# Storing weight blocks earlier and in larger pieces, and loading shared keys once, in a fused attention and MLP kernel

## The chip, the cores and the metric

The kernel runs on one core of a Trainium2 chip. The metric is device time in microseconds of one execution, as a median of several. TensorE (PE), VectorE (DVE), ScalarE (ACT), GpSimd (POOL) and SyncE (SP) each run their instructions in the order in which they were written into the program; SP does nothing here but issue transfers.

## The reference

Chunked attention, with 4 batches, 8 heads, 768 positions and 64 columns a head, is followed by a two-layer MLP over the 3072 tokens.

```python
for c in range(S // 32):                 # chunks of 32 queries
    lo, hi = max(0, 32*c - 16), min(S, 32*c + 32 + 8)
    k_full = concat([mem_k, k[:, :, lo:hi]])      # 8 memory keys and up to 56 neighbours
    a = softmax(q_c @ k_full.T / 8)               # + 1e-9 in the denominator
    out_c = a @ concat([mem_v, v[:, :, lo:hi]])
x = out.reshape(3072, 512)
y = (s * relu(x @ w_in)**2 + b) @ w_out           # 512 -> 2048 -> 512
```

Inputs and outputs are fp32 (the weights arrive as 64-bit floats and are cut down on the chip). Products are formed from a high and a low part of each operand, with three matmuls for one product.

## The kernel before, in words

**Attention.** A *visit* handles six pairs of (block of 64 queries, pair of heads). It loads `raw` (queries and keys, line 506) and `v` (values, line 511), makes scores on TensorE (line 520), takes maxima and exponentials (lines 595 and 599), normalizes on POOL (608 to 611), transposes (632 on DVE, or 620 on TensorE for early visits) and multiplies with the values (line 559). There are 32 visits; each block carries its own copy of its 96 keys, 88 of its window and 8 of memory, so that a pair takes 64 + 96 columns. Visits 0 to 11 serve three token groups of 384; the other 20 serve two groups of 960 tokens, and their results are stored to `xs` (line 570).

**First MLP part.** 48 steps, each with 12 matmuls of the first layer (`hidden`, line 677) and 9 of the second (`result`, line 707), run over the three small token groups. Meanwhile the 32 weight tiles are loaded, decoded and cut into high and low parts (lines 648 to 662), and stay in SBUF.

**Second MLP part.** The two groups of 960 tokens use Strassen-Winograd products: `seven` (line 896) for the first layer and `rest` (line 1018) for the second, once for each group. They need blocks of the weights (A11, A12, A22) and sums of blocks (S1 to S4). These are put together in DRAM, in `w1s` and `w2s`, as 56 *words* each, and a word holds two blocks with their high and low parts, 512 KB. `whole_blocks` lists 48 stores of single blocks (256 KB each); `save` (line 755) issues three of them after each step above 24. `blocks` makes the four sums of a pair of weight tiles on POOL (lines 766 and 774), cuts them on ACT and DVE (777 and 778), and stores them (line 784) with one transfer of 128 KB for each sum and part, eight for a pair of tiles and 128 in all. The buffers `words` (four) hold the sums until their stores have landed. Both kinds of store read `all_w`, the last weight tiles, so none starts before the weights are done. `word` (line 874) reads the words back. `mix` makes the operands B11, B21, B22 and T1 to T4 of each large group from `xs` (loads on line 835, cuts on lines 845 and 846, subtractions on 850).

**Order.** The program is written out by a planner. Each operation has an engine, a holding time and a priority, which is a step number plus an entry of the table `NUDGE`; a list scheduler lays them out against a model of the engines and of the transfers (sizes over `RATE`, at most `FLIGHT` = 8 in flight). What comes out is the fixed order of each engine's instructions. All transfers but one are on SP's queue, in that order.

Of the kernel before, what the change touches and what calls it, by code (L numbers as in the profile page):

```python
# [11 lines left out]
F32 = mybir.dt.float32  # L12
# [9 lines left out]
B, H, S, D = 4, 8, 768, 64  # L22
# [18 lines left out]
QKB = QB + KB  # L41
# [6 lines left out]
LATER = 24.0  # L48
LATE_SUMS = 3
NUDGE = {  # L50
# [69 lines left out]

KINDS = list(dict.fromkeys(k for _, combos in VIEWS for k in kinds_of(combos)))
AT_V = 1024
# [4 lines left out]
BLOCKS = ("A11", "S2", "S1", "S3", "A12", "S4", "A22")  # L127
# [17 lines left out]
STORE, ROWS = 0.85, 1.2  # L145
# [200 lines left out]
def body(ctx: ExitStack, tc: tile.TileContext, qkv, w1, w2, out):  # L346
    nc = tc.nc
    dram = ctx.enter_context(tc.tile_pool(name="dram", bufs=1, space=bass.MemoryType.DRAM))
    w1s = [dram.tile([P, 2, 2, 2 * P], F32, name=f"w1s{i}") for i in range(NWORDS)]
    w2s = [dram.tile([P, 2, 2, 2 * P], F32, name=f"w2s{i}") for i in range(NWORDS)]  # L350
# [35 lines left out]
    raws = ring("raw", 2, [P, GP * QKB], F32)  # L386
# [95 lines left out]
    def attend(vis):  # L482
# [4 lines left out]
        nj, qk, tok = nb // 2, nb * QKB, nb * QB  # L487
# [5 lines left out]
        if vis >= H // 2:  # L493
            raw, v = Val(raws), Val(vs_)
        else:
            raw = Early(NEARLY - 1 - c, 0, GB * QKB)
            v = Early(NEARLY - 5 - c, 0, 2 * GB * D)
# [3 lines left out]
        pieces = (3, 3)[vis] if vis < 2 else 1  # L501
        piece = lambda j: raw[j * pieces // nj]
        first = (lambda: raw.tile) if vis else (lambda: early_tiles[NEARLY - 1])
        for n in range(pieces):
            lo, hi = n * qk // pieces, (n + 1) * qk // pieces + 2 * (not vis and n == pieces - 1)
            op("SP", "issue", a - 4 + load, lambda lo=lo, hi=hi: nc.sync.dma_start(first()[:, lo:hi], qkv[vis][:, lo:hi]), (), (raw[n],),
               size=ROWS * P * (hi - lo) * 4)
# [6 lines left out]
        def product(j):  # L514

            for u in range(2):
                lo = (2 * j + u) * QKB
                for n in range(2):
                    rows = slice(n * D, (n + 1) * D)
                    nc.tensor.matmul(scv(n, j)[u * QB:(u + 1) * QB], raw.tile[rows, lo:lo + QB], raw.tile[rows, lo + QB:lo + QKB],  # L520
                                     start=True, stop=True)
# [40 lines left out]
        def store():  # L562
            if ch is None:
                op("ACT", "xhigh", due + late, lambda: nc.scalar.activation(x.tile[:, :tok], av(), AF.Copy), (va[0],), (x[0],))
                cs, gg = [list(dict.fromkeys(k[i] for k in combos)) for i in range(2)]
                p, lo = divmod(gg[0] - NPLAIN * GB, PB)
                lo, n = lo * QB, len(gg) * QB
                key, i = (p, cs[0] // 2), cs[0] % 2
                staged[key].append((lo, lo + n, vis))
                op("SP", "issue", due + late, lambda: nc.sync.dma_start(  # L570
                    xs[key][:, i:i + len(cs), lo:lo + n], x.tile[:, :tok].rearrange("q (c t) -> q c t", c=len(cs))), (x[0],),
                   (c_xs[key][vis],), size=ROWS * P * tok * 4)
                return
            op("ACT", "xhigh", due + late, lambda: nc.scalar.activation(x.tile[c][:, 0], av(), AF.Copy), (va[0],), (x["H", c],))
            op("DVE", "xlow", due + late, lambda: nc.vector.tensor_tensor(x.tile[c][:, 1], av(), x.tile[c][:, 0].bitcast(F32), ALU.subtract),
               (va[0], x["H", c]), (x["L", c],))
# [93 lines left out]
    def hidden(u):  # L670
# [25 lines left out]
        if u > LATER:  # L696
            save(u, o)

    def result(u):
# [9 lines left out]
        for t in range(NT):  # L709
# [17 lines left out]
            op("SP", "issue", u, lambda ot=ot, row=row: nc.sync.dma_start(out[row:row + P, :], ot()), (o[0],), (), size=ROWS * P * DM * 4)  # L727
# [6 lines left out]
    def save(u, after):  # L734

        for side, unit, q, fn, reads in keep[:3]:
            o = op("SP", "issue", u, fn, reads, (c_ws[side][unit][q, 0],), size=STORE * P * 4 * P * 4)
            o.deps.add(after)
        del keep[:3]
# [4 lines left out]
    def whole_blocks(side, g):  # L744

        fs = (2 * g, 2 * g + 1)
        parts = [[c_w[side, f]["H"], c_w[side, f]["L"]] for f in fs]
        for name in BLOCKS:
            if name in SUMS:
                continue  # L750
            unit, q = place(side, g, name)
            i, k = int(name[1]) - 1, int(name[2]) - 1
            if side:
                i, k = k, i
            keep.append((side, unit, q, lambda unit=unit, q=q, i=i, k=k: nc.sync.dma_start(  # L755
                (w1s, w2s)[side][unit][:, q], weight_tile(side, fs[i])[:, :, k * 2 * P:(k + 1) * 2 * P].bitcast(F32)), [*parts[i], *all_w]))

    def blocks(side, g, due):
# [21 lines left out]
        for name in SUMS:  # L780
            unit, q = place(side, g, name)
            i = where[name]
            for a, v in enumerate((high, sums)):
                op("SP", "issue", due + 0.5, lambda unit=unit, q=q, a=a, v=v, i=i: nc.sync.dma_start(  # L784
                    (w1s, w2s)[side][unit][:, q, a], at(v, i)), (v[0] if v is high else v[i],), (c_ws[side][unit][q, a],), size=STORE * P * 2 * P * 4)
# [82 lines left out]
    def word(p, n, prio):  # L868
        v = Val(streams)
        side, unit = divmod(n, NWORDS)  # L870
        src, c_src = (w1s, w2s)[side][unit], c_ws[side][unit]
        gone = first("stream", stream_slots)
        flat = src.rearrange("p a b n -> p (a b n)")
# [5 lines left out]
    def seven(p, g):  # L879
# [30 lines left out]
        b5 = product("P5", "S1", "T1", 2)  # L910
        sz = Val(wvs, "sz")
        op("DVE", "addp", due - AHEAD, lambda: nc.vector.tensor_tensor(sb(sz), pt(b5), sb(su), ALU.add), (b5[0], su[0]), (sz[0],))
        b7 = product("P7", "S3", "T3", 3)
# [19 lines left out]
    def rest(p):  # L933
# [39 lines left out]
        def out_(m, i, k, due, bank, v=None, add=None, parts=1):  # L973
# [14 lines left out]
            for x in range(parts):  # L988
# [3 lines left out]
                    dst[at:at + P, lo:hi], o.tile[:, lo:hi]), (o[x],), (), size=ROWS * P * (hi - lo) * 4)  # L992
# [143 lines left out]
```

## Time and profile before

| | |
|---|---|
| median of 3 runs | 583.51 us |
| lowest and highest | 582.13 and 585.71 us |
| the profiled execution's own time | 585.3 us |
| its span, first to last instruction | 583.5 us |
| mean granted TensorE clock | 0.994 |
| busy share | PE 98%, DVE 73%, ACT 67%, POOL 34% |
| moved by DMA | 148.08 MB |

The span is what the trace resolves; 1.8 us of the profiled execution's time lie outside it. The profiled execution is near the slow end of the three runs. A step of the first MLP part is a unit of the planner's priorities.

### The profile page before, as it was taken

To read this page: it belongs to the slowest core of one execution; us is meant where nothing else is said; L and a number is where in the kernel's file an instruction comes from. 1 tells how busy PE (TensorE), PEld (TensorE's weight loads), DVE (VectorE), ACT (ScalarE), POOL (GpSimd) and SP (SyncE) were. 2 spreads that over 40 slices of the span, in tenths; PEclk is the share of its full clock that TensorE was granted. 3 is DMA by queue.
4 is the path that set the end of the run, shared out by engine and by line. 5 is a ranking of instruction groups with operands and counts; after the bars stand their busy time and mean duration, and the time that the engine had idled before them with its cause. 6 is when DMAs were issued, how large, how long until landed. Compare 5 with 4: busy or idle time off the path is not lost.

```text
span 583.5 us, 11567 instructions
## 1 busy us (share of the span) xinstructions
PE 570.3 (98%) x3963; PEld 485.5 (83%) x3963; DVE 424.5 (73%) x1117; ACT 393.1 (67%) x950; POOL 196.9 (34%) x230
## 2 busy tenths in 40 slices
PE   7999999999999999899999999999999999999997
PEld 4688888988888788688888888888888888888886
DVE  5889899647968577958988577999734434399653
ACT  6899999667785577857587857675525564655552
POOL 4466354877743468610782212000000101100000
PEclk9999999999999999979999999999999999999999
DMA  8967665148999999996999978767776656666761
GB/s 293 405 256 258 234 211 177 38 154 265 338 328 357 366 308 314 332 322 248 317 370 335 309 243 278 231 213 223 238 262 206 212 189 208 192 205 192 242 215 67
DMA packets 71386, 148.08 MB, mean 254 GB/s; under 512 B 7072, under 2 KB 43808, under 8 KB 71328
## 3 DMA queue, kind: packets, MB, share of 16 engines
q1 hardware_dynamic: 71184, 147.23, 75.4%
q8 instruction: 31, 0.51, 0.4%
q14 instruction: 27, 0.22, 0.1%
q10 hardware_dynamic: 144, 0.12, 0.1%
HBM read 107.74 MB, written 39.58 MB: 252 GB/s over the span
## 4 chain that ended last, share of the span: by engine, by line
PE 78%; DMA 7%; DVE 4%; ACT 3%; SPq 3%; POOL 2%; issue 1%; DVEq 0%; POOLq 0%; ACTq 0%
PE ps L896 25%; PE ps L1018 25%; PE ps L677 11%; PE ps L707 11%; DMA w1s<-w 5%; PE ps L559 3%; PE ps L520 2%; ACT t L599 2%; DVE aT L632 1%; SPq L755 1%; POOL words L774 1%; DMA v<-qkv 1%; DMA w1s<-words 1%; POOL t L611 1%; SPq L784 1%
## 5 line engine op out<-in xcount | busy, mean ns | idle before, releaser
L896 PE MATMUL ps<-again,again 128*128 128x480 f32 x672 | 148.8, 381 | 0.0
L896 PEld LDWEIGHTS ps<-again,again 128*128 128x128 f32 x672 | 125.6, 188 | 20.8
L677 PE MATMUL ps<-x,w 128*128 128x384 f32 x576 | 112.8, 343 | 0.3 <-POOL w L662 0.3
L677 PEld LDWEIGHTS ps<-x,w 128*128 128x128 f32 x576 | 102.3, 191 | 5.9 <-POOL w L662 0.6
L707 PE MATMUL ps<-w,gH 128*128 128x512 f32 x288 | 90.2, 394 | 0.0
L599 ACT ACTIVATE t<-t,nmax 128x96 f32<-128x96 f32 x192 | 69.6, 366 | 19.0 <-DVE nmax L595 18.5
L1018 PE MATMUL ps<-gH,again 128*128 128x482 f32 x272 | 81.5, 380 | 0.0
L632 DVE STREAM_TRANSPOSE aT<-t 32x192 f32<-32x192 f32 x192 | 70.6, 368 | 13.2 <-POOL t L611 10.3
L707 PEld LDWEIGHTS ps<-w,gH 128*128 128x128 f32 x288 | 54.2, 188 | 10.3
L1018 PE MATMUL ps<-again,again 128*128 128x482 f32 x264 | 62.0, 382 | 0.0
L707 PE MATMUL ps<-w,gL 128*128 128x512 f32 x144 | 58.8, 408 | 1.2 <-DVE gL L694 1.1
L1018 PEld LDWEIGHTS ps<-gH,again 128*128 128x128 f32 x272 | 51.3, 188 | 8.2
L1018 PEld LDWEIGHTS ps<-again,again 128*128 128x128 f32 x264 | 49.7, 188 | 8.1
L774 POOL TENSOR_TENSOR words<-words 128x256 f32<-128x256 f32 x64 | 48.0, 750 | 12.3 <-DVE words L778 6.9
L1018 PE MATMUL ps<-gL,again 128*128 128x482 f32 x136 | 51.7, 380 | 0.0
L766 POOL TENSOR_TENSOR words<-w 128x512 f32<-128x512 f32 x32 | 41.3, 1303 | 23.7 <-DMA w1s<-words 17.4
L595 DVE CUSTOM_DVE_ANT_0 t<-ps,mask 128x96 f32<-128x96 f32 x192 | 38.2, 252 | 14.1 <-PE ps L520 13.5
L662 POOL TENSOR_TENSOR w<-wv,w 128x512 fp32r<-128x512 f32 x28 | 36.2, 1298 | 32.4 <-ACT w L659 17.0
L611 POOL TENSOR_TENSOR t<-t,rden 128x576 f32<-128x576 f32 (+1 forms) x40 | 39.2, 982 | 16.8 <-DVE rden L610 8.0
L694 DVE TENSOR_TENSOR gL<-ps,gH 128x384 fp32r<-128x384 f32 x48 | 26.5, 552 | 19.8 <-ACT gH L693 19.5
L692 ACT ACTIVATE ps<-ps,b_sb,s_sb 128x384 f32<-128x384 f32 x48 | 30.6, 638 | 11.4 <-DVE ps L688 10.6
L931 POOL TENSOR_TENSOR againx<-againx 128x480 f32<-128x480 f32 x4 | 5.4, 1348 | 95.6 <-ACT againx L930 89.2
(105 smaller groups left out, 894.6 us busy)
## 6 DMA issues: line engine op xcount, KB each, us to landing
again<-w1s SPq DMA_DIRECT2D x56, 512.0 KB, 4.5
again<-w2s SPq DMA_DIRECT2D x56, 512.0 KB, 4.2
raw<-qkv SPq DMA_DIRECT2D x28, 480.0 KB, 5.3
words<-w SPq DMA_DIRECT2D x24, 512.0 KB, 4.6
v<-qkv SPq DMA_DIRECT2D x28, 384.0 KB, 5.4
w1s<-words SPq DMA_DIRECT2D x64, 128.0 KB, 3.4
w2s<-words SPq DMA_DIRECT2D x64, 128.0 KB, 4.4
w1s<-w SPq DMA_DIRECT2D x24, 256.0 KB, 5.0
```

The source lines that it names most:

```text
L595: op("DVE", "max", a + 0.1, lambda j=j: nc.vector.tensor_tensor_reduce(t.tile[:, n, j, :], scv(j), mask[:, kinds[j]], -SCALE, 3.0e38, ALU. ...
L599: op("ACT", "exp", a + 0.2, lambda j=j: nc.scalar.activation(t.tile[:, n, j, :], t.tile[:, n, j, :], AF.Exp, bias=nmax()[:, j:j + 1], scal ...
L611: op("POOL", NORM[len(each)], a + 0.25, lambda: nc.gpsimd.tensor_tensor(t.tile[:, heads, :nj], t.tile[:, heads, :nj], rden().unsqueeze(3). ...
L632: nc.vector.transpose(aT.tile[gg, :, :nj, u, c * CHUNK:(c + 1) * CHUNK], t.tile[rows, :, :nj, gg])
L662: op(low, "vsum" if turn_ else "wjoin", due, lambda: e.tensor_tensor(dst(1), v.tile, dst(0).bitcast(F32), ALU.subtract), (v[0], w["H"]), ( ...
L677: nc.tensor.matmul(h.tile[:, :TOK], weight_tile(0, f)[:, wi, c * P:(c + 1) * P], x.tile[c][:, xi], start=(c == 0 and n == 0), stop=(c == N ...
L692: op("ACT", "affine", u - ahead, lambda: nc.scalar.activation(hp(), hp(), AF.Identity, scale=s_sb, bias=b_sb), (c_s[0], c_b[0]), (h[0],))
L707: nc.tensor.matmul(acc.tile, g.tile[gi][:, t * P:(t + 1) * P], weight_tile(1, f)[:, wi, :], start=(first and n == 0), stop=(last and n == 2))
L766: o = op("POOL", "vsum", due, lambda k=k, f=f: nc.gpsimd.tensor_tensor(at(sums, 2 * k, 2), weight_tile(side, f)[:, 0].bitcast(F32), weight ...
L774: op("POOL", "ssum", due, lambda to=to, a=a, b=b, how=how: nc.gpsimd.tensor_tensor(at(sums, to), at(sums, a), at(sums, b), how), [sums[x] ...
L896: nc.tensor.matmul(bank.tile[:, :PT], w.tile[:, lo:lo + P], xv.tile[xi][:, kc], start=(not more and kc == 0 and i == 0), stop=(kc == 1 and ...
L1018: nc.tensor.matmul(sx(bank), w.tile[:, lo:lo + P], cut.tile[xi], start=(first and k == 0), stop=(last and k == 2), skip_group_check=True)
```

## The change

- `raw` packs runs of neighbouring blocks: first the queries of a run, then its keys, of which each block after the first adds only `STEP` = 72 columns (64 and the memory keys). Blocks read overlapping windows of 96 columns. A visit of six blocks in one run has 840 columns (one of two runs of three has 864) instead of 960; visits 0 and 1 are loaded in three runs of two blocks, of 296 columns instead of 320.
- `save` begins at step 14 instead of 25 and issues two stores after a step instead of three.
- The sums go out two or three at a time: for a pair of second-layer tiles S2, S3 and S4 together and S1 alone; for the first layer two and two, or two, one and one. With both parts that is 4 or 6 transfers instead of 8, and 72 instead of 128 in all. For this `w1s` becomes tiles of seven words and `w2s` one tile of 56, and the order of blocks in a first-layer word list swaps S1 and S3.
- `seven` computes product P7 ahead of P5.
- The planner's sizes of transfers lose their factors (1.2 for rows, 0.85 for stores; 1.3 stays on the loads of `mix`), and `NUDGE` is a new table, so that the order on every engine is new.

```diff
+STEP = QB + NMEM
+SAVE, NSAVE = 14, 2
 NUDGE = {
-    ('a', 0): -0.5, ('a', 10): -6, ...  ('m', 1): -4.5, ...
+    ('a', 0): -0.5, ('a', 1): 4.5, ...  ('m', 0): 0.5, ('m', 1): 3.75, ...
 }
+def places(vis):
+    runs = []
+    for i, (c, g) in enumerate(VIEWS[vis][1]):
+        if vis < 2 and i % 2 == 0 or not i or VIEWS[vis][1][i - 1] != (c, g - 1):
+            runs.append([])
+        runs[-1].append(i)
+    q, k, ends, at = {}, {}, [], 0
+    for run in runs:
+        for n, i in enumerate(run):
+            q[i], k[i] = at + n * QB, at + len(run) * QB + n * STEP
+        at = k[run[-1]] + KB
+        ends.append(at)
+    return q, k, ends
-BLOCKS = ("A11", "S2", "S1", "S3", "A12", "S4", "A22")
+BLOCKS = ("A11", "S2", "S3", "S1", "A12", "S4", "A22")
-STORE, ROWS = 0.85, 1.2
+ROWS = 1.3
-    w1s = [dram.tile([P, 2, 2, 2 * P], F32, name=f"w1s{i}") for i in range(NWORDS)]
-    w2s = [dram.tile([P, 2, 2, 2 * P], F32, name=f"w2s{i}") for i in range(NWORDS)]
+    stored = [[dram.tile([n, P, 2, 2, 2 * P], F32, name=f"w{side + 1}s{i}") for i in range(NWORDS // n)] for side, n in ((0, len(BLOCKS)), (1, NWORDS))]
...
-                    nc.tensor.matmul(scv(n, j)[u * QB:(u + 1) * QB], raw.tile[rows, lo:lo + QB], raw.tile[rows, lo + QB:lo + QKB],
+                    nc.tensor.matmul(scv(n, j)[u * QB:(u + 1) * QB], raw.tile[rows, q:q + QB], raw.tile[rows, k:k + KB],
...
-        if u > LATER:
+        if u >= SAVE:
             save(u, o)
...
-        for side, unit, q, fn, reads in keep[:3]:
+        for side, unit, q, fn, reads in keep[:NSAVE]:
...
-        for name in SUMS:
-            unit, q = place(side, g, name)
-            i = where[name]
+        pairs = (("S2", "S3", "S4"), ("S1",)) if side else (("S2", "S4"), ("S3", "S1")) if g % 2 == 0 else (("S2", "S4"), ("S3",), ("S1",))
+        for names in pairs:
+            to, at_ = [place(side, g, n) for n in names], [where[n] for n in names]
+            (u, q), n, step = to[0], len(names), at_[1] - at_[0] if len(names) > 1 else 1
+            t, u = words_at(side, u)
             for a, v in enumerate((high, sums)):
+                if n > 1 and to[1][0] == to[0][0]:
+                    dst = t[u, :, :, a]
+                elif n > 1:
+                    by = to[1][0] - to[0][0]
+                    dst = t[u:u + by * (n - 1) + 1:by, :, q, a].rearrange("u p n -> p u n")
...
-        b5 = product("P5", "S1", "T1", 2)
+        b7 = product("P7", "S3", "T3", 2)
+        b5 = product("P5", "S1", "T1", 3)
...
-        b7 = product("P7", "S3", "T3", 3)
```

## Rows read from the trace of the kernel before

**Rows 1.** Windows by stage: PE, PEld, DVE, ACT, POOL busy; clock, DMA share, GB/s.

```profile
0.00:32.00 32.00, 27.85 (x347) 18.55 (x348) 23.40 (x116) 24.94 (x94) 14.49 (x33) 1.00 0.95 354
32.00:146.00 114.00, 114.00 (x833) 99.83 (x832) 90.39 (x243) 99.50 (x246) 72.92 (x77) 1.00 0.59 194
146.00:236.00 90.00, 87.72 (x832) 75.39 (x832) 66.24 (x244) 62.52 (x196) 52.16 (x62) 1.00 1.00 337
236.00:278.00 42.00, 38.98 (x337) 33.83 (x336) 32.59 (x101) 28.56 (x82) 10.60 (x13) 0.92 0.86 289
278.00:358.00 80.00, 80.00 (x588) 67.68 (x589) 63.12 (x183) 55.13 (x141) 35.23 (x38) 1.00 0.92 311
...
579.70:583.50 3.80, 0.01 (x1) 0.00 (x0) 0.84 (x2) 0.00 (x0) 0.00 (x0) 0.93 0.20 65
```

**Rows 2.** Waits of TensorE: us in total, times, longest.

```profile
PE ps L559 <- DMA v<-qkv: 3.0, 1, 3.0
...
PE ps L559 <- DVE nmax L595: 1.1, 1, 1.1
PE ps L707 <- DVE gL L694: 1.1, 2, 0.8
```

**Rows 3.** Windows of 4 us behind the longest wait.

```profile
248.00:252.00 4.00, 3.47 (x51) 3.16 (x52) 0.77 (x8) 0.89 (x4) 0.83 (x1) 0.55 0.95 327
252.00:256.00 4.00, 4.00 (x15) 3.87 (x14) 3.40 (x14) 1.33 (x7) 0.00 (x0) 0.59 0.97 310
```

**Rows 4.** TensorE's timeline, first-layer groups of matmuls: start, duration.

```profile
101.39 2.25 PE L677 MATMUL ps<-x,w 128*128 128x384 f32 x12
105.57 2.26 PE L677 MATMUL ps<-x,w 128*128 128x384 f32 x12
...
142.37 1.22 PE L677 MATMUL ps<-x,w 128*128 128x384 f32 x6
...
251.18 4.21 PE L677 MATMUL ps<-x,w 128*128 128x384 f32 x12
```

**Rows 5.** The chain that ended last, 135 to 280 us.

```profile
151.47 5.91 DMA w1s<-w
...
188.58 5.80 DMA w1s<-words
...
242.24 6.16 DMA v<-qkv
```

**Rows 6.** POOL's timeline at its longest wait in this stretch.

```profile
194.50 1.29 POOL L766 TENSOR_TENSOR words<-w 128x512 f32<-128x512 f32 x1 [11.13 <-DMA w1s<-words]
```

**Rows 7.** DMA view, 146 to 236 us: issues, KB each, landing time.

```profile
DMA packets 24512, 30.35 MB, mean 337 GB/s; under 512 B 2068, under 2 KB 21427, under 8 KB 24499
...
w1s<-w SPq DMA_DIRECT2D x24, 256.0 KB, 5.0
...
raw<-qkv SPq DMA_DIRECT2D x9, 480.0 KB, 5.3
...
w1s<-words SPq DMA_DIRECT2D x30, 128.0 KB, 4.6
```

**Rows 8.** DMA view, 103 to 146 us.

```profile
DMA packets 5632, 6.68 MB, mean 155 GB/s; under 512 B 620, under 2 KB 4860, under 8 KB 5630
...
w1s<-words SPq DMA_DIRECT2D x34, 128.0 KB, 1.9
```

**Rows 9.** POOL's and SP's timelines: last weight tile, first whole-block store.

```profile
101.41 1.30 POOL L662 TENSOR_TENSOR w<-wv,w 128x512 fp32r<-128x512 f32 x1 [1.76 <-ACT w L659]
...
146.30 1.92 SPq L755 DMA_DIRECT2D w1s<-w  x3
```

**Rows 10.** DVE's and TensorE's timelines at the head of `seven`.

```profile
277.91 1.15 DVE L846 TENSOR_TENSOR again<-words,again 128x960 fp32r<-128x960 f32 x1
...
277.90 12.02 PE L896 MATMUL ps<-again,again 128*128 128x480 f32 x54
```

**Rows 11.** DVE busy in the last window of the first `rest`.

```profile
420.00:433.00 13.00, 5.91 (x10) 1.00 0.71 244
```

More of the change, by code (lines that the diff above doesn't have):

```diff
@@ L40 @@
 BLKS = B * NBLK
-QKB = QB + KB
+STEP = QB + NMEM
 SCALE = 0.125
@@ L118, in kinds_of @@
     return [(edge(combos[i][1]), edge(combos[i + 1][1])) for i in range(0, len(combos), 2)]
+def places(vis):
[11 more added lines that the diff above has]
+    return q, k, ends
 KINDS = list(dict.fromkeys(k for _, combos in VIEWS for k in kinds_of(combos)))
-AT_V = 1024
+AT_V = 896
 COLS = AT_V + GP * 2 * D
@@ L348, in body, with words_at @@
     dram = ctx.enter_context(tc.tile_pool(name="dram", bufs=1, space=bass.MemoryType.DRAM))
-    w1s = [dram.tile([P, 2, 2, 2 * P], F32, name=f"w1s{i}") for i in range(NWORDS)]
-    w2s = [dram.tile([P, 2, 2, 2 * P], F32, name=f"w2s{i}") for i in range(NWORDS)]
+    stored = [[dram.tile([n, P, 2, 2, 2 * P], F32, name=f"w{side + 1}s{i}") for i in range(NWORDS // n)] for side, n in ((0, len(BLOCKS)), (1, NWORDS))]
+    def words_at(side, unit):
+        n = NWORDS // len(stored[side])
+        return stored[side][unit // n], unit % n
     xs = {(p, i): dram.tile([P, 2, 2 * PT], F32, name=f"xs{p}_{i}") for p in range(NPAIR) for i in range(NC_T // 2)}
@@ L385, in body @@
     words = ring("words", 4, [P, 2 * DM], F32)
-    raws = ring("raw", 2, [P, GP * QKB], F32)
+    raws = ring("raw", 2, [P, max(places(n)[2][-1] for n in range(H // 2, len(VIEWS)))], F32)
     ts_ = ring("t", 2, [P, 2, GP // 2, KB], F32)
@@ L486, in attend @@
         nb = len(combos)
-        nj, qk, tok = nb // 2, nb * QKB, nb * QB
+        nj, tok = nb // 2, nb * QB
+        q_at, k_at, ends = places(vis)
+        qk = ends[-1]
         c = vis % (H // 2)
@@ L495, in attend @@
         else:
-            raw = Early(NEARLY - 1 - c, 0, GB * QKB)
+            raw = Early(NEARLY - 1 - c, 0, qk)
             v = Early(NEARLY - 5 - c, 0, 2 * GB * D)
@@ L500, in attend @@
         load, late = NUDGE.get(("l", vis), 0.0), NUDGE.get(("x", vis), 0.0) + 0.9
-        pieces = (3, 3)[vis] if vis < 2 else 1
+        pieces = len(ends) if vis < 2 else 1
         piece = lambda j: raw[j * pieces // nj]
@@ L504, in attend @@
         for n in range(pieces):
-            lo, hi = n * qk // pieces, (n + 1) * qk // pieces + 2 * (not vis and n == pieces - 1)
+            lo, hi = (ends[n - 1] if n else 0, ends[n] + 2 * (not vis and n == pieces - 1)) if pieces > 1 else (0, qk)
             op("SP", "issue", a - 4 + load, lambda lo=lo, hi=hi: nc.sync.dma_start(first()[:, lo:hi], qkv[vis][:, lo:hi]), (), (raw[n],),
-               size=ROWS * P * (hi - lo) * 4)
+               size=P * (hi - lo) * 4)
         if not vis:
@@ L516, in product @@
             for u in range(2):
-                lo = (2 * j + u) * QKB
+                q, k = q_at[2 * j + u], k_at[2 * j + u]
                 for n in range(2):
                     rows = slice(n * D, (n + 1) * D)
-                    nc.tensor.matmul(scv(n, j)[u * QB:(u + 1) * QB], raw.tile[rows, lo:lo + QB], raw.tile[rows, lo + QB:lo + QKB],
+                    nc.tensor.matmul(scv(n, j)[u * QB:(u + 1) * QB], raw.tile[rows, q:q + QB], raw.tile[rows, k:k + KB],
                                      start=True, stop=True)
@@ L571, in store @@
                     xs[key][:, i:i + len(cs), lo:lo + n], x.tile[:, :tok].rearrange("q (c t) -> q c t", c=len(cs))), (x[0],),
-                   (c_xs[key][vis],), size=ROWS * P * tok * 4)
+                   (c_xs[key][vis],), size=P * tok * 4)
                 return
@@ L726, in result @@
             row = ch * TOK + t * P
-            op("SP", "issue", u, lambda ot=ot, row=row: nc.sync.dma_start(out[row:row + P, :], ot()), (o[0],), (), size=ROWS * P * DM * 4)
+            op("SP", "issue", u, lambda ot=ot, row=row: nc.sync.dma_start(out[row:row + P, :], ot()), (o[0],), (), size=P * DM * 4)
     c_ws = [[fixed() for _ in range(NWORDS)] for _ in range(2)]
@@ L734, in save @@
     def save(u, after):
-        for side, unit, q, fn, reads in keep[:3]:
-            o = op("SP", "issue", u, fn, reads, (c_ws[side][unit][q, 0],), size=STORE * P * 4 * P * 4)
+        for side, unit, q, fn, reads in keep[:NSAVE]:
+            o = op("SP", "issue", u, fn, reads, (c_ws[side][unit][q, 0],), size=P * 4 * P * 4)
             o.deps.add(after)
-        del keep[:3]
+        del keep[:NSAVE]
     def place(side, g, name):
@@ L755, in whole_blocks @@
             keep.append((side, unit, q, lambda unit=unit, q=q, i=i, k=k: nc.sync.dma_start(
-                (w1s, w2s)[side][unit][:, q], weight_tile(side, fs[i])[:, :, k * 2 * P:(k + 1) * 2 * P].bitcast(F32)), [*parts[i], *all_w]))
+                words_at(side, unit)[0][words_at(side, unit)[1], :, q], weight_tile(side, fs[i])[:, :, k * 2 * P:(k + 1) * 2 * P].bitcast(F32)), [*parts[i], *all_w]))
     def blocks(side, g, due):
@@ L779, in blocks @@
            (high[0],), every, lock=True)
-        for name in SUMS:
-            unit, q = place(side, g, name)
-            i = where[name]
-            for a, v in enumerate((high, sums)):
-                op("SP", "issue", due + 0.5, lambda unit=unit, q=q, a=a, v=v, i=i: nc.sync.dma_start(
-                    (w1s, w2s)[side][unit][:, q, a], at(v, i)), (v[0] if v is high else v[i],), (c_ws[side][unit][q, a],), size=STORE * P * 2 * P * 4)
+        pairs = (("S2", "S3", "S4"), ("S1",)) if side else (("S2", "S4"), ("S3", "S1")) if g % 2 == 0 else (("S2", "S4"), ("S3",), ("S1",))
[3 more added lines that the diff above has]
+            t, u = words_at(side, u)
+            for a, v in enumerate((high, sums)):
+                if n > 1 and to[1][0] == to[0][0]:
[3 more added lines that the diff above has]
+                    dst = t[u:u + by * (n - 1) + 1:by, :, q, a].rearrange("u p n -> p u n")
+                else:
+                    dst = t[u:u + 1, :, q, a].rearrange("u p n -> p u n")
+                op("SP", "issue", due + 0.5, lambda dst=dst, from_=lambda v=v, lo=at_[0], hi=at_[0] + step * (n - 1) + 1, step=step:
+                   v.tile.rearrange("p (i n) -> p i n", i=4)[:, lo:hi:step]: nc.sync.dma_start(dst, from_()),
+                   [v[0]] if v is high else [v[i] for i in at_], [c_ws[side][place(side, g, x)[0]][place(side, g, x)[1], a] for x in names],
+                   size=n * P * 2 * P * 4)
     def again(half, f, shape, dtype):
@@ L870, in word @@
         side, unit = divmod(n, NWORDS)
-        src, c_src = (w1s, w2s)[side][unit], c_ws[side][unit]
+        c_src = c_ws[side][unit]
         gone = first("stream", stream_slots)
-        flat = src.rearrange("p a b n -> p (a b n)")
+        t, u = words_at(side, unit)
+        flat = t[u].rearrange("p a b n -> p (a b n)")
         op("SP", "issue", prio - 3.0, lambda: nc.sync.dma_start(v.tile.bitcast(F32), flat), list(c_src.parts.values()), [v[0], *gone], size=P * DM * 8)
@@ L991, in out_ @@
                 op("SP" if x == parts - 1 else "ACT", "issue", due, lambda eng=eng, lo=lo, hi=hi: eng.dma_start(
-                    dst[at:at + P, lo:hi], o.tile[:, lo:hi]), (o[x],), (), size=ROWS * P * (hi - lo) * 4)
+                    dst[at:at + P, lo:hi], o.tile[:, lo:hi]), (o[x],), (), size=P * (hi - lo) * 4)
         kept = {}
@@ L1114 @@
     for i, (_, combos) in enumerate(VIEWS):
-        n = len(combos) * QKB
-        views[i, :, :n + 2] = np.concatenate([x[g, c] for c, g in combos for x in (qb, kb)] + [sb], axis=-1)
+        q_at, k_at, ends = places(i)
+        for n, (c, g) in enumerate(combos):
+            q, k = q_at[n], k_at[n]
+            views[i, :, q:q + QB] = qb[g, c]
+            if n and k_at[n - 1] == k - STEP:
+                views[i, :, k + LEFT:k + KB] = kb[g, c][:, LEFT:]
+            else:
+                views[i, :, k:k + KB] = kb[g, c]
+        views[i, :, ends[-1]:ends[-1] + 2] = sb
         views[i, :KB, AT_V:] = np.stack([vb[g, c] for c, g in combos], axis=2).reshape(KB, 2 * len(combos) * D)
```

49 rows, old and new, of the table NUDGE are left out of this document.

## Prediction, made before the changed kernel was run

> **What bounds the kernel now.** I read the windows by stage first [rows 1]. TensorE is busy without a gap from 32 to 146 us, from 278 to 358 us, and on to 579.7 us. Its idle time sits in four places: 32.00 - 27.85 = 4.2 us at the start, 90.00 - 87.72 = 2.3 us between 146 and 236 us, 42.00 - 38.98 = 3.0 us between 236 and 278 us, and 3.8 us after the last matmul. So TensorE sets the end, and an edit is worth what it takes from those gaps. Nothing that shortens work on DVE, ACT, POOL or the DMA engines in a stage without gaps can pay.
>
> The waits of TensorE name the gaps of the middle [rows 2]: 3.0 us for a load of `v`, 1.1 us for maxima on DVE, 1.1 us in two pieces for a low part on DVE. Behind the 3.0 us the granted clock is 0.55 and 0.59 in two windows of 4 us, in which TensorE is busy for 3.47 and 4.00 us [rows 3]: it runs at 1.2 GHz, the lower of its two levels, for most of them. The work lost is 0.45 x 3.47 + 0.41 x 4.00 = 3.2 us; twelve first-layer matmuls show it directly, 4.21 us at 251 us against 2.25 us [rows 4]. The shorter gaps leave the clock at 1.00 [rows 1]. The middle thus costs 2.3 + 3.0 + 3.2 = 8.5 us.
>
> Why those gaps? The same table shows DMA at a share of 1.00 and 337 GB/s between 146 and 236 us, after 0.59 between 32 and 146 us [rows 1]. The chain that ended last runs there through transfers, not through TensorE: stores of whole blocks take 5 to 6 us each from issue to landing, a store of sums 5.80 us, and the late `v` 6.16 us [rows 5]. POOL waits 11.13 us for the store at 188.58 us to free a `words` buffer [rows 6], and ACT, which cuts the sums that come from POOL in one order with the parts of the steps, has to wait with it; I read the two shorter kinds of gap as followers of that. So all the gaps of the middle have one cause: the queue of transfers is full there.
>
> **The stores moved.** The whole blocks are 48 x 256 KB = 12.6 MB, and today all go out between 146.3 us and the 236 us window's end [rows 7, 9] (the row of the first layer stands for both). They need the last weight tile, which POOL finishes at 101.41 + 1.30 = 102.7 us [rows 9]. Which step is that? The first store follows step 25, whose products begin at 142.37 us; nine steps of 4.18 us (105.57 - 101.39) and 3.4 us for the two visits between them lead back to 101.4 us, so step 16 begins there [rows 4]. Step 14 is then ahead of the weights by two steps; its stores wait for them, and the planner's list puts them behind the weights. By step 25 the new rule releases 12 x 2 = 24 stores. So 24 x 0.262 = 6.3 MB leave the full stretch for 103 to 146 us, where 6.68 MB go now in 43 us [rows 8]: with them 13 MB, or about 300 GB/s, below the 337 GB/s of the full stretch. The cover is thin but there: TensorE has no gap at a share of 0.92 between 278 and 358 us either [rows 1]. Cost there: none; if the cover fails, sums land late, not at the 1.9 us of today [rows 8] but at 4.6 us [rows 7], and POOL runs behind by 3 us a pair of tiles, which nothing on TensorE needs before 278 us.
>
> What is queued behind a store on SP is the next load, so each store that waits delays a visit's `raw` or `v`. With two a step instead of three this gets less, not more.
>
> **The stores joined.** 128 transfers of sums become 72 at equal bytes. Between 146 and 236 us, 54 of the 132 issues in that view are such stores, 30 to the first tensor and 24 more to the second [rows 7]. Eight in flight at about 4.8 us allow 150 issues in 90 us, so the queue is near that limit as well. After: 24 whole blocks, some 30 sums, the 30 others: 84. The joined stores have a form that no row shows, with two or three rows of 1 KB of one partition that lie far apart in DRAM. Bounds: 4.6 us, as the 128 KB store, and 5.3 us, as a load of 480 KB [rows 7]. I take 5.0 us, the 256 KB store, since most of them carry 256 or 384 KB. None of this is on TensorE's path unless the queue fills.
>
> **The keys loaded once.** A run of six blocks saves 120 columns of 512 bytes, 61 KB. Nine such loads in the full stretch [rows 7] save 0.55 MB. The stretch thus carries 30.35 - 6.29 - 0.55 = 23.5 MB, which at 337 GB/s is 70 of its 90 us, a share of 0.78. At the start visits 0 and 1 save 24 columns a piece, 6 x 12 KB = 74 KB: 0.2 us at 354 GB/s [rows 1], if the pieces arrive sooner by that much. The matmuls keep their shapes; that windows of keys overlap in SBUF costs reads nothing that I can name: 0, with 0.2 us to either side.
>
> **P7 ahead of P5.** P7 needs T3. Its cut on DVE ends at 277.91 + 1.15 = 279.06 us [rows 10]. The run of products at 277.90 us starts with the second one, P6, at 12.02 / 54 x 6 = 1.3 us a product, so P7 would come at 279.2 us: just in time. Cost 0, and at most the one product of 1.3 us. P5's sum and the next one on DVE follow each other more closely, beside products; 0.
>
> **The new order.** `NUDGE` moves loads, visits, stores and cuts on every engine, and no row of before shows the outcome. From below: a gain at the start, where 4.2 us of gaps stand, of at most 2 us. From above: one new gap like the longest, 3.0 + 3.2 = 6.2 us. I take 1.6 us of loss, two gaps like the larger of the low-part waits, 0.8 us [rows 2], as the old order too had gaps where its model had none, and the share that caused them falls.
>
> **The sum.** Against the profiled execution: 585.3 - 8.5 - 0.2 + 1.6 = 578.2 us. The median of before is 583.5 us, 1.8 us below that execution, and so is likely to have had less of the 8.5 us in it; the sum is about work left over and is not shifted again. The gain on the median is 5.3 us, 0.9%. If every gap of the middle goes, 585.3 - 8.7 = 576.6 us; below that only a better start can bring it. One per cent, 5.8 us, is about what a measurement of this kernel can tell from no change, and it lies at 577.7 and 589.3 us.
>
> **Rivals.**
> *The gap moves.* A load or a sum in the new order comes late once, in any stage, and the clock falls with it: 578.2 + 6.2 = 584.4 us. For it: one late `v` did this before, and 278 to 358 us is already at a share of 0.92 [rows 1]. Against it: 20% less to carry in the stretch where it happened. Chance 0.20.
> *The whole blocks do not move.* They may stand in SP's list behind loads, and the weights end two steps after step 14 anyway. Then only joined stores and shorter loads help, some 0.55 MB of 30 [rows 7], and the gaps shrink by a third: 585.3 - 3 = 582 us. Against it: SP has room, as DMA is at 155 GB/s there [rows 8]. Chance 0.08.
> *The joined stores are slow.* If rows of one partition that lie far apart halve the rate, the triples and strided pairs, about 8 MB up to 278 us, take 24 us more of DMA time at 337 GB/s [rows 1], which eats the 20 us that the stretch gains; the gaps come back: 583.5 us. No row of before has such a store. Chance 0.05. The Trainium skill, "DMA: Bandwidth & Descriptors", section "Latency and other measured facts", reports copies whose rows lie a large power of two apart as slower, 164 GB/s at a pitch of 2 MiB against 214 GB/s with the pitch padded; 2 MiB is also the distance between the rows of a triple here. It measured the pitch from partition to partition, which stays 4 KB in this kernel, and no run here shows it. By that rule, an estimate from the page, 7 of the 20 us go, and the time would be about 581 us.
> *The second `mix` starts late: slower.* Its priority moves from 10.5 to 2.25 steps ahead of the second `seven`, that is from 44 to 9.4 us at 4.18 us a step [rows 4]. It needs a load of some 6 us [rows 5], and seven cuts and four subtractions of 1.15 us on DVE [rows 10], 12.7 us: a chain of 19 us. If it started only 9.4 us ahead, TensorE would wait 10 us and then lose 3.2 us of clock: 578.2 + 13 = 591 us. It decides from a start after about 414 us. Against it: a priority is not a time, DVE stands free for 7.1 of the last 13 us before 433 us [rows 11], and the planner gives a free engine whatever is ready. Chance 0.07.
>
> **How the numbers follow.** The forecast, gaps of the middle mostly gone, has 0.60, and its own range is 575 to 581 us. Of it a little over half lies above 577.7 us. Faster by over 1%: about 0.28, and 0.04 more for a better start, 0.32. Slower by over 1%: the late `mix` and two gaps at once, 0.09. The rest, 0.59, is within 1%. The range reaches down to 574.5 us (all gaps gone and 2 us at the start) and up to 586 us, so that it takes in the moved gap; outside remain the late `mix`, double gaps and a few per cent below.
>
> **What would show it.** Right: first whole-block stores at 103 to 107 us; DMA share near 0.85 between 103 and 146 us and near 0.8 between 146 and 236 us; POOL's waits for stores gone; no wait of TensorE over 1 us between 146 and 278 us, and the clock at 1.00 throughout; no gap at P7. Wrong: stores of sums that land later than 5.3 us, a wait for `v` or `raw` in another place with a clock of 0.6 behind it, idle time at the head of the second `seven`, or a start longer than 32 us.

## The result, and the profile after

The changed kernel takes 577.34 us as a median of 7 runs (576.89 to 578.52); the kernel before takes 582.15 us in its 7 runs (580.17 to 585.71). The ratio is 0.9917 with a 95% interval of 0.989 to 0.9943: faster by 0.8%, and steadier, with a spread of 1.6 us against 5.5 us. The profiled execution took 578.52 us, with a span of 576.7 us, 6.8 us less than before. The fall of the clock behind the late `v` is not in every execution of the kernel before: of the 35 beside the runs `b_keys` to `a_split` below, 18 show a mean granted clock of 0.999 or 1.000, with a median of 581.9 us, and 17 one of 0.994 to 0.998, with 583.6 us.

The windows by stage of the changed kernel, to be laid beside [rows 1] (columns as there; 32 to 146 us is cut in two at 103 us):

```profile
0.00:32.00 32.00, 27.70 (x336) 18.63 (x341) 22.98 (x118) 24.64 (x93) 14.36 (x33) 1.00 0.95 353
32.00:103.00 71.00, 68.64 (x485) 59.26 (x485) 63.67 (x159) 68.19 (x164) 37.16 (x36) 1.00 0.60 203
103.00:146.00 43.00, 43.00 (x310) 38.29 (x310) 24.82 (x71) 30.28 (x81) 33.53 (x39) 1.00 0.82 266
146.00:236.00 90.00, 89.74 (x840) 78.31 (x836) 70.93 (x248) 65.91 (x203) 59.54 (x67) 1.00 1.00 324
236.00:278.00 42.00, 42.00 (x363) 36.09 (x362) 36.45 (x110) 30.37 (x85) 16.07 (x18) 1.00 0.76 255
278.00:358.00 80.00, 80.00 (x610) 67.49 (x609) 62.58 (x182) 56.69 (x144) 26.38 (x31) 1.00 0.87 287
```

TensorE's gaps of the middle fell from 2.3 + 3.0 us to 0.26 + 0 us, and the clock stays at 1.00 where it was 0.92. New gaps of 2.4 us stand between 32 and 103 us. Its waits, beside [rows 2]:

```profile
PE ps L546 <- DMA early<-qkv: 2.7, 3, 1.3
PE ps L646 <- POOL t L637: 0.9, 1, 0.9
...
PE ps L703 <- DVE wv L681: 0.6, 1, 0.6
...
PE ps L733 <- POOL w L688: 0.5, 1, 0.5
PE ps L733 <- DVE gL L720: 0.3, 1, 0.3
```

No `v` and no maxima are waited for any more. What is left belongs to the first loads, to the decoding of weights, and, with 0.9 us at 34.94 us, to probabilities that POOL normalizes (`t`) for an early visit. POOL's own waits for stores of sums fell too, first before, then after:

```profile
POOL words L766 <- DMA w1s<-words: 17.4, 3, 11.1
```

```profile
POOL words L792 <- DMA w1s<-words: 1.7, 1, 1.7
```

On SP's timeline the whole blocks start at 101.73 us, 44.6 us earlier than in [rows 9]. On POOL's, the last weight tile is not done until 103.41 + 1.30 = 104.71 us, so here they start ahead of it and not behind it:

```profile
101.73 7.17 SPq L781 DMA_DIRECT2D w1s<-w  x10
```

```profile
103.41 1.30 POOL L688 TENSOR_TENSOR w<-wv,w 128x512 fp32r<-128x512 f32 x1 [1.75 <-ACT w L685]
```

The DMA view from 103 to 146 us, where [rows 8] had 6.68 MB, and then that from 146 to 236 us, beside [rows 7]:

```profile
DMA packets 10528, 11.44 MB, mean 266 GB/s; under 512 B 706, under 2 KB 9925, under 8 KB 10523
...
w1s<-w SPq DMA_DIRECT2D x20, 256.0 KB, 3.9
w1s<-words SPq DMA_DIRECT2D x12, 256.0 KB, 2.9
```

```profile
DMA packets 22593, 29.14 MB, mean 324 GB/s; under 512 B 1645, under 2 KB 19178, under 8 KB 22581
...
w2s<-w SPq DMA_DIRECT2D x24, 256.0 KB, 5.2
...
w2s<-words SPq DMA_DIRECT2D x10, 384.0 KB, 5.3
raw<-qkv SPq DMA_DIRECT2D x8, 420.0 KB, 5.3
w1s<-words SPq DMA_DIRECT2D x12, 256.0 KB, 4.9
...
w2s<-words SPq DMA_DIRECT2D x10, 128.0 KB, 5.2
```

The early stretch filled nearly as forecast, with 20 of the 24 stores, but the full one did not empty: 29.14 MB instead of 30.35. Sums (20 transfers to each tensor, 9.4 MB against 54 x 0.131 = 7.1 MB) and the first three words read back moved up into the room; the last sum is stored from 298.4 us on instead of 316.9 us, and the shares after 236 us are lower instead (0.76 and 0.87 against 0.86 and 0.92).

### The profile page after: what moved, and what is told of

Same layout as the page of the kernel before. It is cut to its first block, busy times and chain, and to the rows that moved or that the text cites. A ratio compares the mean times of both kernels' runs of the same rounds, so it can differ in the third digit from the quotient of the medians.

```text
span 576.7 us, 11446 instructions
## 1 busy us (share of the span) xinstructions
PE 565.7 (98%) x3950; PEld 482.2 (84%) x3954; DVE 430.3 (75%) x1117; ACT 393.0 (68%) x950; POOL 197.6 (34%) x230
## 4 chain that ended last, share of the span: by engine, by line
PE 86%; POOL 4%; ACT 3%; DVE 2%; issue 2%; DMA 2%; SPq 0%; DVEq 0%; POOLq 0%; ACTq 0%
PE ps L1056 26%; PE ps L934 26%; PE ps L733 14%; PE ps L703 13%; PE ps L585 3%; PE ps L546 3%; POOL words L800 2%; POOL words L792 1%; ACT t L625 1%; DMA raw<-qkv 1%; DMA early<-qkv 1%; PE ps L646 1%; ACT ps L676 1%; POOL t L637 1%; ACT w L685 1%
## 5 line engine op out<-in xcount | busy, mean ns | idle before, releaser
L703 PE MATMUL ps<-x,w 128*128 128x384 f32 x576 | 111.4, 339 | 1.2 <-DVE wv L681 0.6
L703 PEld LDWEIGHTS ps<-x,w 128*128 128x128 f32 x576 | 100.6, 188 | 6.9 <-POOL w L688 0.7
L1044 DVE TENSOR_TENSOR gL<-again,gH 128x480 fp32r<-128x480 f32 x43 | 30.2, 712 | 10.3 <-ACT gH L1043 9.8
```

The lines of the kernel that those rows point to most:

```text
L703: nc.tensor.matmul(h.tile[:, :TOK], weight_tile(0, f)[:, wi, c * P:(c + 1) * P], x.tile[c][:, xi], start=(c == 0 and n == 0), stop=(c == N ...
L1044: op("DVE", "lowp", due - AHEAD, lambda cut=cut, v=v: nc.vector.tensor_tensor(cut.tile[1][:, :PT], at(v), cut.tile[0][:, :PT].bitcast(F32) ...
```

## The experiments

All eleven kernels keep the order of TensorE, DVE, ACT and POOL of the kernel that they start from, instruction for instruction. Where the keys alone are edited SP's order stays too; joined and split stores stand in the places of those that they replace. So an edit of the transfers is seen without the reordering that a planner would add. Whole blocks are moved in the finished list; each run has its own numbers where `first` and `each` stand:

```diff
     laid = plan.lay((lambda t: spare and t < 40e3, warm))
+    laid = place_stores(laid, stores, step_end, first, each)
...
+def place_stores(laid, stores, step_end, first, each):
+    mine = {o for o, _ in stores}
+    rest = [x for x in laid if x[2] not in mine]
...
+    for i, (o, after) in enumerate(stores):
+        low = max([low, at[step_end[first + i // each]]] + [at[d] for d in o.deps if d is not after])
...
+        behind.setdefault(low, []).append((0.0, o.n, o))
```

Ratios are to the kernel before on the same chip, with 95% intervals; labels that begin with b start from the kernel before, those with a from the changed one. Of the columns, *whole blocks* gives the step behind which their stores begin and how many follow each step; *sums* are stored joined or each by its own transfer (joined makes 72 transfers in the changed kernel, 80 in `b_all` and `b_join`); *keys* are loaded once for neighbouring blocks, or each block has its own copy.

| label | whole blocks | sums | keys | median us | ratio |
|---|---|---|---|---|---|
| the change | step 14, two | joined | once | 577.34 | 0.9917 [0.989, 0.9943] |
| b_early | step 14, two | single | own | 578.47 | 0.9935 [0.9923, 0.9948] |
| b_all | step 14, two | joined | once | 579.19 | 0.9951 [0.9937, 0.9965] |
| a_late | step 25, three | joined | once | 584.75 | 1.0047 [1.0034, 1.006] |
| a_none | step 25, three | single | own | 594.12 | 1.0208 [1.019, 1.0226] |
| b_keys | step 25, three | single | once | 580.03 | 0.9975 [0.9944, 1.0005] |
| b_join | step 25, three | joined | own | 583.05 | 1.0006 [0.998, 1.0031] |
| a_keys | step 14, two | joined | own | 578.26 | 0.9927 [0.9905, 0.9949] |
| a_split | step 14, two | single | once | 579.94 | 0.9962 [0.9939, 0.9984] |
| b_early_keys | step 14, two | single | once | 577.89 | 0.9903 [0.9866, 0.994] |
| b_24_2 | step 24, two | single | own | 588.21 | 1.0073 [1.0047, 1.01] |
| a_three | step 14, three | joined | once | 580.0 | 0.9949 [0.9922, 0.9976] |

My theory was that the full queue of transfers made the gaps (theory 1); the rival was that the new order of the compute engines made the gain (theory 2).

**b_early** (`first = 14, each = 2` on the kernel before).

> The kernel before, with the order on TensorE, DVE, ACT and POOL kept instruction for instruction; on SP alone the 48 whole-block stores move to two after each step from step 14 on (behind the weights). Theory 1, the transfers: the full queue between 146 and 236 us made the gaps of the middle, and moving 24 of the stores to 103 to 146 us takes most of them: 578 to 579.5 us, TensorE idle under 2 us between 146 and 278 us. Theory 2, the order: the new order of the compute engines made the gain, and the stores alone do nothing: within 1 us of the kernel before, about 582 us.

Measured 578.47 us. The windows of 103 to 278 us, then TensorE's waits:

```profile
103.00:146.00 43.00, 43.00 (x337) 38.19 (x336) 26.49 (x77) 29.94 (x77) 34.01 (x40) 1.00 0.85 285
146.00:236.00 90.00, 89.05 (x840) 76.88 (x839) 68.33 (x260) 64.52 (x203) 54.36 (x64) 1.00 0.92 297
236.00:278.00 42.00, 42.00 (x364) 36.09 (x363) 38.11 (x110) 30.83 (x86) 14.87 (x18) 1.00 0.88 293
```

```profile
PE ps L726 <- DVE gL L712: 0.9, 1, 0.9
```

The gaps of the middle go from 5.3 to 0.95 us with no compute instruction moved. Theory 1 holds: the stores alone give 0.65% where the whole change gives 0.83%, and the two intervals overlap. What is left is a wait for a low part on DVE (`gL`), of the kind that took 1.1 us before.

**b_all** (the same, with joined sums and packed keys).

> The kernel before with the order of its compute engines kept and all three edits of the transfers made: whole blocks from step 14 two a step, sums stored three or two at a time (S1 and S3 of the first layer still alone, so 80 transfers instead of 72), neighbouring keys loaded once. Theory 1, the transfers: 577 to 578.5 us, as the changed kernel. Theory 2, the order: 581 to 582 us.

Measured 579.19 us, 0.7 us above the expectation and no better than `b_early`: no gain of the other two edits together is seen in the old order. The expectation of theory 2 is missed by more.

**a_late** (`first = 25, each = 3` on the changed kernel).

> The changed kernel with the order of its compute engines kept; only the whole-block stores go back to three after each step from step 25 on. Theory 1, the transfers: the gaps come back, at least one of them long enough to lower the clock: 581 to 584 us. Theory 2, the order: 578.5 us at most.

Measured 584.75 us, 0.75 us above the range expected and slower than the kernel before. The windows, and then TensorE's timeline where it waits:

```profile
103.00:146.00 43.00, 43.00 (x337) 38.20 (x336) 25.70 (x75) 29.74 (x77) 33.97 (x40) 1.00 0.45 147
146.00:236.00 90.00, 84.69 (x749) 73.01 (x749) 65.68 (x226) 59.21 (x174) 57.24 (x64) 1.00 1.06 350
```

```profile
194.31 0.50 PE L752 MATMUL ps<-w,gL 128*128 128x512 f32 x1 [0.87 <-DVE gL L738]
...
221.58 0.50 PE L752 MATMUL ps<-w,gL 128*128 128x512 f32 x1 [1.31 <-DVE gL L738]
...
235.58 0.92 PE L603 MATMUL ps<-aT,v 96*64 96x64 f32 x24 [1.60 <-DVE nmax L639]
...
237.17 3.79 PE L721 MATMUL ps<-x,w 128*128 128x384 f32 x12
```

The gaps are back, 5.3 us of them, all in the full stretch and behind DVE, as the two shorter kinds of [rows 2] were; behind the last, twelve matmuls take 3.79 us. POOL's waits for stores are back as well, 10.2 us in total.

**a_none** (all three edits undone, order of the change).

> The changed kernel with the order of its compute engines kept and all three edits of the transfers undone: whole blocks from step 25 three a step, one transfer for each sum and part, a copy of its keys for each block. Theory 1, the transfers: 582 us or more, as before or worse, since this order was laid out for lighter transfers. Theory 2, the order: 578.5 us at most.

Measured 594.12 us: the new order with the old transfers is 2.1% slower than the old order with them. So the new order is no gain by itself; it only fits lighter transfers. Undoing the keys and the joined sums together with the whole blocks costs 594.12 - 584.75 = 9.4 us more than undoing the whole blocks alone, while `a_keys` and `a_split` below lie 0.9 and 2.6 us above the change: the prices of the three edits do not add up. Its largest wait, behind which the clock is 0.61 and 0.54 in two windows of 4 us:

```profile
PE ps L610 <- DVE nmax L646: 5.9, 1, 5.9
```

**b_keys** (only the packed keys, every order kept).

> The kernel before, every order kept, SP's too; only the loads of raw are the packed ones (840 columns instead of 960). Theory 1, the transfers, by bytes: 0.55 of 30 MB leave the full stretch, 2%, so at most 1 us: 581 to 582 us. Rival, the gap at the start hangs on the first loads: 0.3 us less there at once. A gain above 2 us would mean that bytes and not the place of the stores decide.

Measured 580.03 us, below the 581 to 582 us expected, with an interval that reaches from 0.9944 to past 1. Its last sentence stays undecided: the medians differ by 582.70 - 580.03 = 2.7 us, the ratio gives 0.25%, 1.5 us. The gap before `v` is in its profile, but that is the slowest of its 12 executions (585.93 us; the fastest took 577.68), so the gap shows nothing about the others:

```profile
PE ps L579 <- DMA v<-qkv: 2.8, 1, 2.8
```

**b_join** (only the joined sums; where `left` names of a group are still to come, nothing is issued):

```diff
+                def store(a=a, v=v, group=group, left=left):
+                    left.pop()
+                    if left:
+                        return
...
+                    dst = t[u:u + by * (n - 1) + 1:by, :, q, a].rearrange("u p n -> p u n")
```

> The kernel before, every compute engine's order kept; sums stored two or three at a time, each joined store in the place of the last one that it stands for (80 instead of 128; S1 and S3 of the first layer alone). Theory 1a, the count of transfers fills the queue (132 issues in 90 us, eight in flight): 579 to 580.5 us. Theory 1b, the bytes fill it: within 1 us of before, or up to 1 us slower, since the early pieces wait for the last one.

Measured 583.05 us, 1.0006: the number of transfers did not fill the queue in the old order. (Eight in flight is a number of the planner's model; no run shows it as a limit.)

**a_keys** (the change, with own keys for each block).

> The changed kernel with every order kept and each block given its own copy of its keys again (960 columns). If bytes are covered now: within 0.7 us of the changed kernel, 577.3 to 578.2 us. If its queue is still at the limit between 146 and 236 us (the share is 1.00 there in its profile): 579 to 581 us.

Measured 578.26 us, at the edge of the first case: 0.9 us above the change, which the intervals don't separate. The DMA share between 146 and 236 us is 1.01, and TensorE's gaps there are 0.2 us: a full share that nobody waits behind cost nothing here.

**a_split** (the change, with a transfer for each sum and part again).

> The changed kernel with every order kept and each sum and part stored by its own transfer again, 128 instead of 72, in the places of the joined ones. If only the whole blocks matter: within 1 us of the changed kernel. If the count of transfers matters in this order (undoing everything cost 9 us more than undoing the whole blocks): 580 to 585 us, with waits for words buffers on POOL.

Measured 579.94 us, between the two cases, 2.6 us above the change; the intervals overlap a little. Its waits of the middle, of which the change has none but 0.3 us:

```profile
PE ps L733 <- DVE gL L720: 1.6, 1, 1.6
PE ps L585 <- DVE nmax L621: 1.1, 1, 1.1
...
PE ps L585 <- DVE aT L658: 0.9, 1, 0.9
```

They are waits for DVE and not for a transfer, but POOL, whose results DVE waits for, stands before stores of sums again, for 8.6 us instead of 1.7 us:

```profile
POOL words L792 <- DMA w2s<-words: 4.4, 2, 4.1
POOL words L792 <- DMA w1s<-words: 4.2, 2, 2.3
```

So by their profiles joined stores have a use in the new order, which was laid out for them; in the time the intervals still touch. In the old order no use is seen.

**b_early_keys** (`b_early` with packed keys).

> The kernel before, compute order kept, with the whole blocks moved to two a step from step 14 and the packed raw loads, but sums stored singly. Joining alone gave nothing in the old order and the three edits together (0.9951) no more than the moved blocks alone (0.9935). If the keys add their own part (0.9975 alone) to the moved blocks: 577 to 578 us, as the changed kernel, so that the new order is worth nothing. If the moved blocks had taken all that is to be had in this order: 578 to 579 us, as with the moved blocks alone.

Measured 577.89 us, ratio 0.9903: as good as the change, with the old order of the compute engines and single sums. That the keys add a part to `b_early` is likely by the two ratios, but not shown: their intervals overlap.

**b_24_2** (`first = 24, each = 2` on the kernel before).

> The kernel before, compute order kept, the whole blocks two a step but from step 24 only, so that they end at step 47 instead of 40: the rate of the new kernel without its early start. If the rate of three a step fills the queue: 578.5 to 580 us. If it is the early start (bytes that have to pass between 146 and 278 us): the gaps stay, 581 to 583 us, or worse, since stores now stand ahead of the loads of 236 to 278 us.

Measured 588.21 us. That is 5 us above the range of the second case, its "or worse". The full stretch is relieved, the next one is not; windows, then the longest wait:

```profile
146.00:236.00 90.00, 89.16 (x842) 77.11 (x841) 68.99 (x262) 64.61 (x203) 54.68 (x64) 1.00 0.93 307
236.00:278.00 42.00, 36.41 (x284) 30.68 (x285) 29.77 (x87) 26.68 (x76) 8.69 (x12) 0.92 1.01 347
```

```profile
PE ps L916 <- ACT wv L926: 3.4, 1, 3.4
```

The slower rate alone pushes the stores into 236 to 278 us (12 whole blocks are issued there instead of one), where the share rises from 0.86 to 1.01 and the gaps from 3.0 to 5.6 us. The slower rate does not pay without the early start.

**a_three** (`first = 14, each = 3` on the changed kernel).

> The changed kernel, compute order kept, the whole blocks three a step from step 14, so that all are out by step 29. If more room between 146 and 236 us still pays: 576 to 577 us. If what is left of the gaps is elsewhere (2.4 us between 32 and 103 us, none over 0.3 us after that): within 0.7 us of the changed kernel. If the stores now delay sums and loads between 103 and 146 us: 578.5 to 581 us.

Measured 580.0 us, the third case by its time. DMA is at 0.98 between 103 and 146 us, and two gaps appear, but later:

```profile
103.00:146.00 43.00, 43.00 (x336) 38.14 (x335) 26.78 (x84) 29.54 (x75) 33.97 (x40) 1.00 0.98 329
```

```profile
166.58 0.92 PE L603 MATMUL ps<-aT,v 96*64 96x64 f32 x24 [1.68 <-DMA v<-qkv]
195.28 0.50 PE L752 MATMUL ps<-w,gL 128*128 128x512 f32 x1 [1.62 <-DVE gL L738]
```

Between 146 and 236 us the share is 0.89, lower than the 1.00 of the change, and the gaps are 3.3 us instead of 0.26 us: a load of `v` comes late, behind stores of whole blocks and sums that the chain shows from 139.80 to 158.89 us. That two a step is the better rate is likely but not clear of noise, as the intervals overlap (0.9949 against 0.9917).

## Why the prediction held, step by step

The forecast of 578.2 us stands against 577.34 us measured, and the gain of 5.3 us against 582.15 - 577.34 = 4.8 us. That the sum came out so close is in part luck. It starts from an execution near the slow end and books 3.2 us for a fall of the clock that about half of the executions before don't show; the prediction says itself that the median is likely to have less of it. Put into the same sum, what the two profiles show gives 585.3 - 8.2 + 2.4 = 579.5 us; the profiled execution took 578.52 us, so 1 us of the gain stands in no term.

**The 8.5 us of the middle.** Right in place and size: 0.26 us of gaps are left and the clock stays at 1.00, so 8.2 us of the profiled execution are gone. That the whole-block stores in the queue made most of them is shown, not only argued: moving them alone takes 4.4 of the 5.3 us of gaps in the old order (`b_early`), and moving them back puts 5.0 us of gaps into the new one (`a_late`). "One cause" was too much. TensorE's timeline before has the shorter gaps here, and the chain leads from POOL's late buffer, at 194.50 us in [rows 6], to the maxima (`nmax`) that the second of these two waits for:

```profile
193.26 0.50 PE L707 MATMUL ps<-w,gL 128*128 128x512 f32 x1 [0.83 <-DVE gL L694]
...
205.06 0.92 PE L559 MATMUL ps<-aT,v 96*64 96x64 f32 x24 [1.12 <-DVE nmax L595]
```

```profile
197.49 1.12 POOL t L611
198.63 0.37 DVE aT L632
```

It runs over POOL's normalizing and DVE's transposes, and not over ACT's cuts as I had it. The gap of 0.83 us comes before POOL has its buffer, so it does not follow from that; one of 0.86 us for the same low part stays in `b_early`. What makes it is open.

**The share of 0.78.** Wrong, without effect on the time. I counted what leaves the stretch and not what moves into it: the new order puts sums and reads of words into the room, and the share is 1.00. Where the order is kept it falls (0.92 in `b_early`), though less than I had it. The step that failed is the one from "less to carry" to "a lower share". Nor does the share tell of gaps: 1.00 goes with 0.26 us of gaps in the change and 0.89 with 3.3 us in `a_three`. What counted in these runs is whether a transfer that is waited for stands behind ones that are not. POOL's waits for stores nearly went, as forecast, but not by the stores' move alone: `b_early` still has 12.6 us of them, with 0.95 us of gaps on TensorE.

**The loss of 1.6 us for the new order.** Measured 2.4 us, between 32 and 103 us, where [rows 1] had none. The size was half as large again, and the place was not foreseen. Three of the four gaps, 1.5 us, are for weights whose decoding now runs late; the fourth, 0.9 us, is for probabilities on POOL. POOL's timeline and TensorE's show one of the three:

```profile
69.69 2.53 POOL L688 TENSOR_TENSOR w<-wv,w 128x512 fp32r<-128x512 f32 x2 [6.50 <-ACT ps L676]
```

```profile
71.03 0.73 PE L733 MATMUL ps<-w,gH 128*128 128x512 f32 x2 [0.45 <-POOL w L688]
```

**The start, 0.2 us.** TensorE's idle time there is 4.3 us instead of 4.2 us; waits for the first pieces rose from 2.1 to 2.7 us, and by 32 us both kernels have run the same 24 matmuls of the first layer. No gain is seen.

**The joined stores.** I took 5.0 us between 4.6 and 5.3 us; in the full stretch the triples land in 5.3 us and the pairs in 4.9 us. The triples, with rows 2 MiB apart, land no later than loads of 420 KB (5.3 us) and hardly later than single sums of 128 KB to the same tensor (5.2 us). From 236 to 300 us they land in 7.2 us, which the prediction named as a sign of slow stores, but single sums take 7.0 us there too: it is the stretch and not the form. So the rival of slow stores finds no support. The rule of the Trainium skill, "DMA: Bandwidth & Descriptors", section "Latency and other measured facts", is on the pitch from partition to partition, and the trace has no sign that it reaches this form (its 214 GB/s were measured at 4 MiB + 4 KiB). As landing times in a full queue hardly depend on the size here, they are a weak test of the rate.

**P7 ahead of P5.** 0 was right: no wait of TensorE is on a first-layer product of the large groups.

**The rivals.** No gap moved to a place where it takes the clock. The whole blocks did move, from 101.73 us on, ahead of the 103 to 107 us named. The late `mix` was close: in the new order the last subtraction and cut before the second `seven` run from 420.69 us on, where the old order had its last at 392.21 us, and they end 1.7 us before TensorE begins that product. DVE's timeline, and the chain:

```profile
420.69 1.15 DVE L887 TENSOR_TENSOR words<-words,words 128x960 f32<-128x960 f32 x1
422.91 1.16 DVE L883 TENSOR_TENSOR again<-words,again 128x960 fp32r<-128x960 f32 x1 [1.07 <-ACT again L882]
```

```profile
425.76 73.33 PE ps L934 x336
```

**What stays open.** Whether the new order is worth anything: `b_early_keys` reaches the same time without it, within intervals of 0.3 to 0.4% to either side. How much the packed keys give, since `b_keys` did not decide it. And whether another order would win back the 2.4 us between 32 and 103 us; none was tried.

## What to carry to other kernels

Where the bound engine waits behind a queue of transfers, first look for traffic that nobody waits for soon, and for the earliest moment at which its data is ready; moving it into an idle stretch paid 0.65% here without touching a compute instruction. A slower rate from nearly the same start only moved the collision. A DMA share of 1.00 says little by itself: the question is what stands ahead of the load that is waited for.

An order laid out for one set of transfers can be far worse with another (2.1% here), so test an edit of the traffic in a fixed order before crediting either one.

## What was not expected of the hardware

The clock's fall does not go by the length of a gap alone. A wait of 1.60 us at 235.58 us in `a_late` is followed by twelve matmuls in 3.79 us, and one of 1.68 us at 166.58 us in `a_three` leaves the clock at 1.00. Windows of 2 us behind each, `a_late` first:

```profile
236.00:238.00 2.00, 2.00 (x45) 1.72 (x41) 0.61 (x3) 2.00 (x11) 0.00 (x0) 0.73 1.10 310
238.00:240.00 2.00, 2.00 (x8) 2.00 (x7) 1.04 (x12) 1.59 (x8) 1.00 (x2) 0.50 1.04 298
```

```profile
168.00:170.00 2.00, 2.00 (x18) 1.79 (x11) 1.86 (x14) 2.00 (x7) 1.25 (x2) 1.00 0.93 259
```

The two windows of `a_late` lose (0.27 + 0.50) x 2 = 1.5 us of work, and none is lost in `a_three`; in two of the five executions of `a_late` the mean clock is 1.000. So in these runs a gap of 1.6 to 1.7 us cost once or twice its size, and a forecast should carry both.
